# The first batch of a threshold-attention and GELU kernel: divisors through DRAM, conversions counted per slot, and two steps moved

## The chip, the cores and the metric

The kernel runs on one core of one Trainium2 chip. The metric is the device time of one execution in microseconds (us); all times below are us unless they are marked ns. A core has TensorE (PE; its weight loads are listed apart as PEld), VectorE (DVE), ScalarE (ACT), GpSimd (POOL), SyncE (SP, which here only issues DMAs) and 16 DMA engines. [...]

## The reference

```python
# q, k, v: (8, 8, 576, 64) float32; w_in: (512, 2048), w_out: (2048, 512), both float64
scores = (1 / 8) * q @ k.transpose(0, 1, 3, 2)
thresh = scores.max(-1, keepdims=True) - tau
scores = where(scores >= thresh, scores, -1e9)
attn = exp(scores - scores.max(-1, keepdims=True))
attn = attn / (attn.sum(-1, keepdims=True) + 1e-9)
x = (attn @ v)          # to rows of tokens: (4608, 512)
h = x @ w_in
out = (0.5 * h * (1 + erf(h / sqrt(2)))) @ w_out
```

The two weight matrices come as 64-bit floats, and the kernel makes 32-bit floats of them on the chip.

## The kernel before, in words

**Pairs, chunks and slots.** Two heads make a pair; there are 8 batches of 4 pairs, 32 in all. The 576 rows of a pair are cut into five chunks: four of 128 rows for each of the two heads, and a last one that holds the 64 remaining rows of both. One (pair p, chunk i) is a slot n. The first batch (pairs 0 to 3, slots 0 to 19; `BATCH` is 20) has an order of its own: first chunks 0 and 1 of all four pairs (slots 0 to 7), then chunks 2, 3, 4 of each pair (slots 8 to 19). From slot 20 on it is pair by pair. The order on each engine is the order in which this Python program emits the instructions; there is no scheduler (`manual_schedule`).

**A slot of the first batch.** `scores` (L408) lets PE write the scores into one or two of the two PSUM tiles `sc`. `softmax_head` takes the negated row maximum on DVE (L420), on POOL the threshold `thr` (L423) and on ACT the exponentials `p` (L425). `softmax_tail` lets DVE drop what is under the threshold and sum up the rows (L441, the sums go to `den`), which frees the PSUM tile for the scores of the next slot; POOL adds 1e-9 to the sums (L444). One slot later, DVE inverts the sums (`invert`, L450) and PE transposes `p` (`turn_p_early`, L354) through PSUM into pT, which ACT copies out (L361, L365, L370, L374). Another slot later, `weigh_v` or `weigh_half` multiplies pT with v into x^T (L544, L568), ACT copies x^T into its block of tokens (L554, L570), and `divide_early` divides: PE spreads the inverted sums over partitions by matmuls with the identity (L463), ACT copies them (L465), POOL multiplies (L471). x^T comes in two parts, columns 0 to 255 (`TOK`) after chunk 1 and columns 256 to 575 after chunk 4. The second part of pairs 0, 1, 2, 3 falls into slots 12, 15, 18 and 21. From batch 1 on, `divisors` does it otherwise: it transposes the sums on DVE (L482), writes them to DRAM (L485) and reads them back spread over partitions (L491, L493), all from SP.

**PSUM.** All other PSUM tiles (tr, xT, hT, o_ps, idle) share one ring of four (tag `mm`); the fifth of them waits until the first has been read.

**Conversions.** The 64-bit weights come in 32 pieces of 128x512 (16 of w_in, then 16 of w_out), loaded by `load_piece` (L183, from SP) into free slots of xall or into parts of turned_p. A piece is converted in two steps: ACT makes the power and the low half (L202, L203), DVE makes the high half (L210, L211), after which the next piece is loaded; later POOL adds the low bits (L224, `add_low_bits`). `conversions` is a generator that has ACT's step one piece ahead of DVE's, and stops ahead of the last two pieces; `convert(ns)` at the end of every slot lets it run for a debt in ns: 0 in slot 0, 1200 in slots 1 and 2, 1900 later, each piece counted as 1060; the last pieces come in slot 19. In fact DVE converts this many in slots 0 to 19:

```
0 2 1 2 1 2 2 2 2 1 2 2 2 1 2 2 2 2 0 2
```

**The other work of the first batch.** From slot 10 (`START`) on, `fill` gives PE matmuls of layer 1 of token block 0 (L636), 6 to 7 a slot by the goal `GOAL`; ACT copies hT (L603), and after slot 20 turns it into GELU (L609); layer 2 of the block (L651) begins in slot 21. q, k and v of pair 4 are loaded in slot 13 (`load(HP)`), those of pair 5 in slot 17. In slots 1, 6, 8 and 20 `keep_busy` gives PE some idle matmuls (L304).

**After the first batch** PE has the attention of the other 28 pairs, mixed with token blocks as filler, and last the ten remaining blocks in a form with fewer products (L824).

Of the kernel before, what the change touches and what calls it, by code (L numbers as in the profile page):

```python
# [8 lines left out]
FP32 = mybir.dt.float32  # L9
U32 = mybir.dt.uint32  # L10
U8 = mybir.dt.uint8
AF = mybir.ActivationFunctionType
# [6 lines left out]
def kernel(  # L19
# [163 lines left out]
        eng.dma_start(raw, src.bitcast(U32))  # L183
        raws.append((dst, raw, slot))

    def conversions():

        vec = nc.vector
        ahead = []
        done = 0
        while raws or ahead:
            if raws:
                dst, raw, slot = raws.pop(0)
                lo, hi = (raw.rearrange("p (f w) -> p f w", w=2)[:, :, i] for i in range(2))  # L200
                power = gp.tile([P, PIECE], U32, tag="g", name="power")
                nc.scalar.activation(power.bitcast(FP32), hi.bitcast(FP32), AF.Copy, bias=0.0, scale=2.0 ** -112)  # L202
                nc.scalar.activation(dst.bitcast(U32), lo, AF.Copy, bias=0.0, scale=2.0 ** -29)  # L203
                ahead.append((dst, hi, power, slot))
                yield 0
            if len(ahead) == LATER and done == len(pieces) - LATER:
                yield None
            if len(ahead) == 2 or not raws:
                dst, hi, power, slot = ahead.pop(0)
                vec.tensor_scalar(power, power, 3, 0x7FFFFFF8, op0=ALU.logical_shift_left, op1=ALU.bitwise_and)  # L210
                vec.scalar_tensor_tensor(power, hi, 0x80000000, power, op0=ALU.bitwise_and, op1=ALU.bitwise_or)  # L211
                x_free.extend(slot)
                sums_due.append((dst.bitcast(U32), power))
                load_piece()
                done += 1
                yield 1060

    sums_due = []

# [4 lines left out]
            nc.gpsimd.tensor_tensor(dst, power, dst, op=ALU.add)  # L224
            converted[0] += 1

    conv = {"steps": None, "debt": 0.0}

    def convert(ns, least=0):

        if conv["steps"] is None:
            conv["steps"] = conversions()
        conv["debt"] += ns
        while conv["debt"] > 0 or least > 0:
            took = next(conv["steps"], None)
            if took is None:
                return
            conv["debt"] -= took
            least -= took


    st = {}
# [2 lines left out]
    def load(p):  # L245
        for _ in load_steps(p):
            pass
# [180 lines left out]
    def softmax_tail(p, i):  # L428

        s = st[p]  # L430
        sc, thr, w = s.pop(("sc", i)), s.pop(("thr", i)), s["p", i]
        n = len(sc)
        if p < EARLY:
            pair = small.tile([P, 2], FP32, tag="den", name="den", bufs=2 * SLOTS)
            den = [pair[:, e:e + 1] for e in range(n)]
        else:
            at = [e * NC + i if i < NC else 2 * NC for e in range(n)]
            den = [sums[p % 2][:, x:x + 1] for x in at]
        for e in range(n):
            row = w[:, e * S:(e + 1) * S].rearrange("p (h s) -> p h s", h=2)  # L440
            nc.vector.scalar_tensor_tensor(  # L441
                row, sc[e][:, :, 0:HALF], thr[:, e:e + 1], row, op0=ALU.is_ge, op1=ALU.mult, accum_out=den[e])
        if p < EARLY:
            nc.gpsimd.tensor_scalar(pair[:, 0:n], pair[:, 0:n], 1e-9, None, op0=ALU.add)  # L444
            s["sum", i] = pair[:, 0:n]

    def invert(p, i):

        den = st[p]["sum", i]
        nc.vector.reciprocal(den, den)  # L450

    def divide_early(p, lo, hi):

# [165 lines left out]
    def table():  # L619

        if dirty[0]:
            nc.scalar.activation(warm[:, 1:2], warm[:, 0:1], AF.Exp)
            dirty[0] = False
# [466 lines left out]
    PARTS = 1.3, 1.3, 0.2, 1.3, 0.9  # L1090

    HALVED = (2, 3)
    BUSY = {1: 2, 6: 2, 8: 2, BATCH: 4}

    tokens = 0
# [4 lines left out]
    for n in range(len(slots) + WEIGH + 1):  # L1100
# [3 lines left out]
        if p < NP:  # L1104
            scores(p, i)
            softmax_head(p, i)
            add_low_bits()
            if last and last[0] < EARLY:
                invert(*last)
            if p < HP - 1 and i == 0:  # L1110
                turn_qk_early(p + 1)
        elif n == len(slots):
            early_end.close()
            weights_first()
        gelus(0)
        if n == BATCH:
            gelus_held()
        table()
        for args in due:
            if len(args) == 2:  # L1120
                weigh_half(*args)
                if args[1]:
                    divide_early(args[0], 0, TOK)
                continue
            weigh_v(*args)
            divide_early(*args)
        due = []
        if p > EARLY and i == WEIGH:
            for lo, hi in (0, WIDE), (WIDE, S):
                weigh_v(p - 1, lo, hi)  # L1130
            if p == NP:
                divide(p - 1)
# [20 lines left out]
        if p < 2 and i == 0:  # L1153
            for _ in range(2):
                load_piece()
            load_v_early(p + 2)
        if p == 1 and i == NC:
            load(HP)
        if n == BATCH - 3:
            load(HP + 1)  # L1160
        if n == BATCH:
# [9 lines left out]
            scale_q(p + 1)  # L1171
        if p >= HP - 1 and i == 2 and p + 1 < NP:
            turn_qk(p + 1)
        convert(0 if n == 0 else 1200 if n < 3 else 1900 if n < BATCH - 1 else 1e9)
        if not early:
            lag[0] = 2 if p < NP else 0
            if n != BATCH:
# [56 lines left out]
```

## Time and profile before

| | |
|---|---|
| runs without profile | median 1337.11 us of 3 (1337.1 to 1337.74) |
| profiled execution | 1337.72 us, its span 1335.9 us |
| PE busy | 1318.8 us, 99% of the span |
| DVE, ACT, POOL busy | 1039.9, 605.8, 637.0 us |
| L210, DVE, first step of the high half | x32, 488 ns mean |
| L211, DVE, second step | 717 to 720 ns mean |
| L202 and L203, ACT | 0.70 us each, starting 0.57 apart |
| L224, POOL, low bits | x32, 1272 ns mean |
| L463, PE, spreading the divisors | 48 of 80 records in slots 12, 15, 18, 21 |
| L465, ACT, their copy | 373 to 465 ns, x8 |
| L471, POOL, the multiplication | 321 to 1087 ns, x12 |
| L450, DVE, inverting | 154 ns mean |

The maximum of the first head of a slot (L420) starts at these times:

| slot | 1 | 2 | 3 | 4 | 5 | 6 | 7 | 8 | 9 | 10 |
|---|---|---|---|---|---|---|---|---|---|---|
| us | 13.86 | 20.00 | 25.89 | 32.75 | 37.58 | 44.53 | 49.96 | 55.93 | 61.35 | 66.25 |
| **slot** | **11** | **12** | **13** | **14** | **15** | **16** | **17** | **18** | **19** | **20** |
| us | 71.69 | 77.12 | 86.51 | 90.74 | 96.87 | 105.34 | 110.34 | 118.13 | 124.48 | 129.22 |

A line of the timeline gives the start, the duration of the group, the engine, the line of the kernel, the operation, what it writes and reads, how often, and in brackets how long the engine had been idle before and what ended that. An instruction that issues a DMA is listed under SPq. One matmul of 32-bit floats makes two records.

### The profile page before, as it was taken

The numbers are of one execution on the slowest core, as the hardware profiler recorded it, in microseconds if no ns is written. First come the engines' busy times: TensorE is split into PE (matmuls) and PEld (weight loads), VectorE is DVE, ScalarE is ACT, GpSimd is POOL, SyncE is SP. The second block draws the span as 40 slices with busy tenths as digits, with TensorE's granted clock in tenths as the row PEclk, the third lists the DMA queues.
The fourth block names the chain that finished last, engine by engine and source line by source line (L and its number), as shares of the span: only waits on it lengthen the run. The fifth ranks groups of instructions, "written<-read, shape, count | busy, mean of one in ns | idle before, by whom it ended". The sixth has DMA issues, their size and how long they took to land.

```text
span 1335.9 us, 19987 instructions
## 1 busy us (share of the span) xinstructions
PE 1318.8 (99%) x6370; PEld 896.2 (67%) x6370; DVE 1039.9 (78%) x2007; ACT 605.8 (45%) x1029; POOL 637.0 (48%) x1066
## 2 busy tenths in 40 slices
PE   8899999999999999999999999999999999999998
PEld 6677466466466466466466557568788787877877
DVE  6877777788888888888888888783857698386775
ACT  7987457258357358348448428232211103211120
POOL 3655454555555556555555541235264503635530
PEclk9999999999999999999999999999999999999999
DMA  7553565776786786786796775400000130000003
GB/s 242 212 148 64 124 151 139 166 186 152 173 191 151 178 203 154 174 221 155 172 219 156 167 188 116 106 9 1 1 0 1 40 103 17 0 1 0 1 0 80
DMA packets 209784, 152.42 MB, mean 114 GB/s; under 512 B 113360, under 2 KB 193088, under 8 KB 209680
## 3 DMA queue, kind: packets, MB, share of 16 engines
q1 hardware_dynamic: 191536, 124.59, 39.6%
q0 software_dynamic: 17712, 26.26, 7.4%
q8 instruction: 52, 0.85, 0.3%
q14 instruction: 52, 0.43, 0.1%
q10 hardware_dynamic: 432, 0.30, 0.1%
HBM read 55.97 MB, written 12.52 MB: 51 GB/s over the span
## 4 chain that ended last, share of the span: by engine, by line
PE 94%; DVE 2%; ACT 2%; issue 0%; DMA 0%; SPq 0%; POOL 0%; ACTq 0%; DVEq 0%
PE bank L824 34%; PE o_ps L651 17%; PE hT L636 16%; PE sc L408 13%; PE xT L544 11%; DVE nmx L420 1%; ACT p L425 1%; PE tr L354 1%; DVE power L211 1%; ACT pT L361 0%; DVE power L210 0%; DVE p L441 0%; DMA q<-in_q_dram 0%; ACT power L202 0%; PE tr L324 0%
## 5 line engine op out<-in xcount | busy, mean ns | idle before, releaser
L425 ACT ACTIVATE p<-sc,nmx 128x576 f32<-128x576 f32 x288 | 201.9, 737 | 279.1 <-DVE nmx L420 278.8
L441 DVE SCALAR_TENSOR_TENSOR p<-sc,thr,p 128x576 f32<-128x576 f32 x288 | 225.6, 816 | 72.9 <-ACT p L425 62.2
L423 POOL TENSOR_SCALAR thr<-nmx,tau_eff 128x1 f32<-128x1 f32 x288 | 84.0, 293 | 335.8 <-DVE nmx L420 331.3
L636 PE MATMUL hT<-xall,w_in 128*128 128x256 f32 x1024 | 242.1, 386 | 0.5 <-ACT g L603 0.5
L420 DVE TENSOR_REDUCE nmx<-sc 128x1 f32<-128x576 f32 x288 | 205.5, 750 | 44.2 <-PE sc L408 42.7
L651 PE MATMUL o_ps<-w_out,g 128*128 128x512 f32 x512 | 236.8, 603 | 0.0
L636 PEld LDWEIGHTS hT<-xall,w_in 128*128 128x128 f32 x1024 | 189.7, 190 | 50.4 <-issue 23.0
L706 DVE TENSOR_TENSOR o<-o,bank 128x256 f32<-128x256 f32 (+1 forms) x242 | 100.2, 417 | 94.4 <-PE bank L824 89.4
L706 DVE TENSOR_TENSOR c<-c,bank 128x320 f32<-128x320 f32 x304 | 147.1, 488 | 33.9 <-PE bank L824 20.5
L651 PEld LDWEIGHTS o_ps<-w_out,g 128*128 128x128 f32 x512 | 93.3, 190 | 108.9 <-issue 106.6
L408 PE MATMUL sc<-kT,qT 64*128 64x288 f32 x960 | 159.6, 431 | 2.1 <-DVE p L441 1.6
L544 PE MATMUL xT<-pT,v 128*64 128x320 f32 (+1 forms) x1240 | 159.7, 411 | 0.6 <-DVE pT L365 0.5
L505 DVE STREAM_TRANSPOSE turned_p<-p 128x1152 f32<-128x1152 f32 x112 | 154.4, 1378 | 3.9
L408 PEld LDWEIGHTS sc<-kT,qT 64*128 64x128 f32 x960 | 91.5, 187 | 74.9 <-issue 59.2
L544 PEld LDWEIGHTS xT<-pT,v 128*64 128x64 f32 x1240 | 86.7, 137 | 71.6 <-issue 10.7
L824 PE MATMUL bank<-w_out,c 128*128 128x256 f32 (+1 forms) x484 | 120.6, 380 | 0.8 <-DVE o L706 0.8
L267 POOL DMA_DIRECT2D v<-in_v_dram x208 | 110.8, 536 | 4.1 <-issue 2.1
L824 PEld LDWEIGHTS bank<-w_out,c 128*128 128x128 f32 x484 | 90.5, 190 | 18.7 <-DVE o L706 3.2
L891 ACT ACTIVATE c<-c 128x320 f32<-128x320 f32 (+1 forms) x80 | 46.9, 624 | 114.6 <-DVE c L706 114.5
L824 PE MATMUL bank<-t_out,g 128*128 128x256 f32 (+1 forms) x324 | 82.5, 377 | 0.4 <-DVE o L706 0.4
L824 PE MATMUL bank<-t_out,c 128*128 128x256 f32 x320 | 82.8, 381 | 0.0
L706 POOL TENSOR_TENSOR c<-c,g 128x320 f32<-128x320 f32 (+1 forms) x40 | 50.5, 1271 | 67.5 <-DVE c L706 67.5
(181 smaller groups left out, 1762.5 us busy)
## 6 DMA issues: line engine op xcount, KB each, us to landing
pT<-turned_p SPq DMA_DIRECT2D x448, 160.0 KB, 3.5
pT<-pd_tail SPq DMA_DIRECT2D x112, 80.0 KB, 2.8
q<-in_q_dram POOLq DMA_DIRECT2D x104, 72.0 KB, 3.8
k<-in_k_dram POOLq DMA_DIRECT2D x104, 72.0 KB, 3.0
inv<-turned SPq DMA_DIRECT2D x54, 128.0 KB, 4.0
v<-in_v_dram POOLq DMA_DIRECT2D x156, 40.0 KB, 3.1
out_dram<-o SPq DMA_DIRECT2D x40, 128.0 KB, 2.3
xall<-in_moe_w_out_dram SPq DMA_DIRECT2D x9, 512.0 KB, 4.2
```

The source lines that it names most:

```text
L267: eng.dma_start(t[r:P:4, e, 0:n, :], rows[:, r * KR:r * KR + n, :])
L408: nc.tensor.matmul(sc[e][:, h, 0:HALF], lhsT=lhsT, rhs=s["kT"][rows, at:at + HALF], start=True, stop=True)
L420: nc.vector.tensor_reduce(nmx[:, e:e + 1], sc, axis=AXIS.XY, op=ALU.max, negate=True)
L423: nc.gpsimd.tensor_scalar(thr[:, e:e + 1], nmx[:, e:e + 1], -1.0, tau_eff, op0=ALU.mult, op1=ALU.subtract)
L425: nc.scalar.activation(w[:, e * S:(e + 1) * S].rearrange("p (h s) -> p h s", h=2), sc, AF.Exp, bias=nmx[:, e:e + 1], scale=1.0)
L441: nc.vector.scalar_tensor_tensor(row, sc[e][:, :, 0:HALF], thr[:, e:e + 1], row, op0=ALU.is_ge, op1=ALU.mult, accum_out=den[e])
L505: nc.vector.transpose(turned_p[:, :, i // 2, 0:NB, i % 2 * Q:(i % 2 + 1) * Q], w.rearrange("p (e b i) -> p e b i", e=2, i=Q))
L544: nc.tensor.matmul(to, lhsT=s["v"][:, e, c, :], rhs=rhs, start=(c == 0), stop=(c == KR - 1))
L636: nc.tensor.matmul(hT[:, j % 2, :], lhsT=w_in_sb[c][:, j * P:(j + 1) * P], rhs=x_blk[n][:, c, :], start=(c == 0), stop=(c == N_DM - 1))
L651: nc.tensor.matmul(o[:, 0:d_model], lhsT=g[j][:, m * P:(m + 1) * P], rhs=w_out_sb[j], start=(j == 0), stop=(j == N_DF - 1))
L706: eng.tensor_tensor(out, a, b, op=ALU.add)
L824: nc.tensor.matmul(to, lhsT=l, rhs=r, start=start and k == 0, stop=k == len(pairs) - 1, skip_group_check=not start)
```

## The change

- **Divisors of the second part through DRAM.** In the first batch, chunks 2, 3 and 4 now sum into columns of `sums` instead of `den`; 1e-9 is added once a pair, after chunk 4. The new `divisors_early(p)`, called in the slot after chunk 4 (slots 11, 14, 17, 20), inverts and transposes the sums on DVE, writes them to DRAM and reads them back spread over partitions with four DMAs, all issued by SP. The target is a part of w_out that is not yet converted for pairs 0 and 1, and the tile `inv` for pairs 2 and 3. The new `divide_late(p)` lets POOL multiply in slots 14, 16, 19 and 22 (`DIVIDE_LATE`). The matmuls of L463 and the copies of L465 for columns 256 to 575 are gone, and `invert` remains for chunks 0 and 1.
- **Conversion steps per slot.** Instead of the debt in ns, a list `STEPS` says how many pieces DVE converts in each slot; ACT is one piece ahead. All 32 are done in slot 18. By the built program DVE's counts in slots 0 to 19 are

```
0 1 1 1 1 1 2 1 2 2 2 2 3 2 2 3 2 2 2 0
```

- **ScalarE's halves sooner in the slots of long x^T.** In slots 12, 15 and 18, `convert_ahead` gives ACT the halves of the slot's pieces (3, 3 and, as only one is left, 1) right after its exponentials and its copy of hT, ahead of the copies of x^T and pT.
- **q and k of pair 4 sooner.** They are loaded in slot 11 (`START + 1`) instead of slot 13, behind the DMAs of `divisors_early(0)`; v stays in slot 13.

The order of TensorE's instructions is otherwise the same in both built programs.

```diff
--- before.py
+++ after.py
@@ -183,37 +183,32 @@
         eng.dma_start(raw, src.bitcast(U32))
         raws.append((dst, raw, slot))
-    def conversions():
+    ahead = []
+    def convert_first():
+        dst, raw, slot = raws.pop(0)
+        lo, hi = (raw.rearrange("p (f w) -> p f w", w=2)[:, :, i] for i in range(2))
+        power = gp.tile([P, PIECE], U32, tag="g", name="power")
+        nc.scalar.activation(power.bitcast(FP32), hi.bitcast(FP32), AF.Copy, bias=0.0, scale=2.0 ** -112)
+        nc.scalar.activation(dst.bitcast(U32), lo, AF.Copy, bias=0.0, scale=2.0 ** -29)
+        ahead.append((dst, hi, power, slot))
+    def convert_second():
         vec = nc.vector
-        ahead = []
-        done = 0
-        while raws or ahead:
-            if raws:
-                dst, raw, slot = raws.pop(0)
-                lo, hi = (raw.rearrange("p (f w) -> p f w", w=2)[:, :, i] for i in range(2))
-                power = gp.tile([P, PIECE], U32, tag="g", name="power")
-                nc.scalar.activation(power.bitcast(FP32), hi.bitcast(FP32), AF.Copy, bias=0.0, scale=2.0 ** -112)
-                nc.scalar.activation(dst.bitcast(U32), lo, AF.Copy, bias=0.0, scale=2.0 ** -29)
-                ahead.append((dst, hi, power, slot))
-                yield 0
-            if len(ahead) == LATER and done == len(pieces) - LATER:
-                yield None
-            if len(ahead) == 2 or not raws:
-                dst, hi, power, slot = ahead.pop(0)
-                vec.tensor_scalar(power, power, 3, 0x7FFFFFF8, op0=ALU.logical_shift_left, op1=ALU.bitwise_and)
-                vec.scalar_tensor_tensor(power, hi, 0x80000000, power, op0=ALU.bitwise_and, op1=ALU.bitwise_or)
-                x_free.extend(slot)
-                sums_due.append((dst.bitcast(U32), power))
-                load_piece()
-                done += 1
-                yield 1060
+        dst, hi, power, slot = ahead.pop(0)
+        vec.tensor_scalar(power, power, 3, 0x7FFFFFF8, op0=ALU.logical_shift_left, op1=ALU.bitwise_and)
+        vec.scalar_tensor_tensor(power, hi, 0x80000000, power, op0=ALU.bitwise_and, op1=ALU.bitwise_or)
+        x_free.extend(slot)
+        sums_due.append((dst.bitcast(U32), power))
+        load_piece()
     sums_due = []
@@ -224,19 +219,17 @@
             nc.gpsimd.tensor_tensor(dst, power, dst, op=ALU.add)
             converted[0] += 1
-    conv = {"steps": None, "debt": 0.0}
-    def convert(ns, least=0):
-        if conv["steps"] is None:
-            conv["steps"] = conversions()
-        conv["debt"] += ns
-        while conv["debt"] > 0 or least > 0:
-            took = next(conv["steps"], None)
-            if took is None:
-                return
-            conv["debt"] -= took
-            least -= took
+    def convert_ahead(steps):
+        while raws and len(ahead) <= steps:
+            convert_first()
+    def convert(steps):
+        while steps > 0 and (ahead or raws):
+            convert_ahead(1)
+            convert_second()
+            steps -= 1
     st = {}
@@ -430,8 +423,8 @@
         s = st[p]
         sc, thr, w = s.pop(("sc", i)), s.pop(("thr", i)), s["p", i]
         n = len(sc)
-        if p < EARLY:
-            pair = small.tile([P, 2], FP32, tag="den", name="den", bufs=2 * SLOTS)
+        if p < EARLY and i < 2:
+            pair = small.tile([P, 2], FP32, tag="den", name="den", bufs=2 * HP)
             den = [pair[:, e:e + 1] for e in range(n)]
         else:
             at = [e * NC + i if i < NC else 2 * NC for e in range(n)]
@@ -440,14 +433,49 @@
             row = w[:, e * S:(e + 1) * S].rearrange("p (h s) -> p h s", h=2)
             nc.vector.scalar_tensor_tensor(
                 row, sc[e][:, :, 0:HALF], thr[:, e:e + 1], row, op0=ALU.is_ge, op1=ALU.mult, accum_out=den[e])
-        if p < EARLY:
+        if p < EARLY and i < 2:
             nc.gpsimd.tensor_scalar(pair[:, 0:n], pair[:, 0:n], 1e-9, None, op0=ALU.add)
             s["sum", i] = pair[:, 0:n]
+        elif p < EARLY and i == NC:
+            at = sums[p % 2][:, 0:2 * NC + 1]
+            nc.gpsimd.tensor_scalar(at, at, 1e-9, None, op0=ALU.add)
     def invert(p, i):
         den = st[p]["sum", i]
         nc.vector.reciprocal(den, den)
+    def divisors_early(p):
+        den = sums[p % 2]
+        nc.vector.reciprocal(den[:, 0:2 * NC + 1], den[:, 0:2 * NC + 1])
+        turned = small.tile([P, Q], FP32, tag="turned", name="turned", bufs=2)
+        nc.vector.transpose(turned, den)
+        rows = dram.tile([4, Q, Q], FP32, tag="turned", name="turned", bufs=4)
+        nc.sync.dma_start(rows.rearrange("a k i -> (a k) i"), turned)
+        t = st[p]["inv"] = w_out_sb[N_DF - 1 - p] if p < 2 else dg.tile([P, S], FP32, tag="inv", name="inv")
+        flat = rows.rearrange("a k i -> a (k i)")
+        for e in range(2):
+            to = t[e * D:(e + 1) * D]
+            src = flat[:, (e * NC + 2) * Q:(e * NC + 4) * Q].unsqueeze(0).to_broadcast([D, 4, 2 * Q])
+            nc.sync.dma_start(to[:, 0:TOK].rearrange("p (a x) -> p a x", x=2 * Q), src)
+            src = rows[2 * e:2 * e + 2, 2 * NC, :].unsqueeze(0).to_broadcast([D, 2, Q])
+            nc.sync.dma_start(to[:, TOK:TOK + TAIL].rearrange("p (a x) -> p a x", x=Q), src)
+    def divide_late(p):
+        b, hp = divmod(p, HP)
+        by = st[p].pop("inv")
+        for n, o, at, size in in_blocks(b, TOK, S):
+            x, y = x_blk[n][:, hp, o:o + size], by[:, at - TOK:at - TOK + size]
+            if size == TOK:
+                x = x.rearrange("q (a i c) -> q a c i", i=Q, c=2)
+                y = y.rearrange("q (a c i) -> q a c i", i=Q, c=2)
+            nc.gpsimd.tensor_tensor(x, x, y, op=ALU.mult)
     def divide_early(p, lo, hi):
@@ -1090,6 +1118,8 @@
     PARTS = 1.3, 1.3, 0.2, 1.3, 0.9
     HALVED = (2, 3)
+    DIVIDE_LATE = {14: 0, 16: 1, 19: 2, 22: 3}
+    STEPS = [0, 1, 1, 1, 1, 1, 2, 1, 2, 2, 2, 2, 3, 2, 2, 3, 2, 2, 2]
     BUSY = {1: 2, 6: 2, 8: 2, BATCH: 4}
     tokens = 0
@@ -1105,8 +1135,10 @@
             scores(p, i)
             softmax_head(p, i)
             add_low_bits()
-            if last and last[0] < EARLY:
+            if last and last[0] < EARLY and last[1] < 2:
                 invert(*last)
+            if last and last[0] < EARLY and last[1] == NC:
+                divisors_early(last[0])
             if p < HP - 1 and i == 0:
                 turn_qk_early(p + 1)
         elif n == len(slots):
@@ -1116,6 +1148,8 @@
         if n == BATCH:
             gelus_held()
         table()
+        if early and n > START and any(hi == S for _, *_, hi in due):
+            convert_ahead(STEPS[n] if n < BATCH - 1 else LATER)
         for args in due:
             if len(args) == 2:
                 weigh_half(*args)
@@ -1123,8 +1157,11 @@
                     divide_early(args[0], 0, TOK)
                 continue
             weigh_v(*args)
-            divide_early(*args)
+            if args[1] == 0:
+                divide_early(*args)
         due = []
+        if n in DIVIDE_LATE:
+            divide_late(DIVIDE_LATE[n])
         if p > EARLY and i == WEIGH:
             for lo, hi in (0, WIDE), (WIDE, S):
                 weigh_v(p - 1, lo, hi)
@@ -1154,8 +1191,13 @@
             for _ in range(2):
                 load_piece()
             load_v_early(p + 2)
-        if p == 1 and i == NC:
-            load(HP)
+        if n == START + 1:
+            loads = load_steps(HP)
+            next(loads)
+            next(loads)
+        if n == START + 3:
+            for _ in loads:
+                pass
         if n == BATCH - 3:
             load(HP + 1)
         if n == BATCH:
@@ -1171,7 +1213,7 @@
             scale_q(p + 1)
         if p >= HP - 1 and i == 2 and p + 1 < NP:
             turn_qk(p + 1)
-        convert(0 if n == 0 else 1200 if n < 3 else 1900 if n < BATCH - 1 else 1e9)
+        convert(STEPS[n] if n < BATCH - 1 else len(pieces))
         if not early:
             lag[0] = 2 if p < NP else 0
             if n != BATCH:
```

## The prediction

> **What bounds the kernel now.** I read the chain of work that ended last, then busy time by stage, then the timeline of the first 142 us.
>
> ```profile
> PE 94%; DVE 2%; ACT 2%; issue 0%; DMA 0%; SPq 0%; POOL 0%; ACTq 0%; DVEq 0%
> ```
>
> TensorE ends the program; the 2% each of DVE and ACT lies early, since in each 20 us from 140 to 300 TensorE is busy for 20.00. By stage (us; then busy time of PE, weight loads, DVE, ACT, POOL; granted clock; DMA share):
>
> ```profile
> 10.00:64.00 54.00, 47.16 (x447) 34.41 (x443) 44.63 (x96) 49.36 (x103) 27.64 (x46) 0.97 0.70 238
> 64.00:128.00 64.00, 61.84 (x369) 47.05 (x368) 46.69 (x99) 49.57 (x102) 33.55 (x53) 1.00 0.47 117
> 128.00:142.00 14.00, 13.31 (x82) 8.18 (x83) 10.24 (x22) 12.31 (x23) 5.33 (x15) 1.00 0.00 0
> ```
>
> From 10 to 64 us (slots 1 to 9) ScalarE has 91% and TensorE has 6.8 us of idle; from 64 us (slots 10 on, with block 0 as filler) TensorE has 97%. Before 64 us an early slot goes like slot 7:
>
> ```profile
> 51.77 0.82 DVE L441 SCALAR_TENSOR_TENSOR p<-sc,thr,p 128x576 f32<-128x576 f32 x1 [0.33 <-POOL thr L423]
> ...
> 52.65 1.97 PE L408 MATMUL sc<-kT,qT 64*128 64x288 f32 x8
> ...
> 53.19 0.74 POOL L471 TENSOR_TENSOR xall<-xall,inv 128x256 f32<-128x256 f32 x1
> ...
> 53.25 0.96 DVE L210 TENSOR_SCALAR power<-power 128x512 uint32<-128x512 uint32 x1
> ...
> 54.25 0.69 DVE L211 SCALAR_TENSOR_TENSOR power<-xall,power 128x512 uint32<-128x512 uint32 x1
> ...
> 54.86 0.42 DVE L210 TENSOR_SCALAR power<-power 128x512 uint32<-128x512 uint32 x1
> ...
> 55.32 0.69 DVE L211 SCALAR_TENSOR_TENSOR power<-turned_p,power 128x512 uint32<-128x512 uint32 x1
> ...
> 55.93 1.41 DVE L420 TENSOR_REDUCE nmx<-sc 128x1 f32<-128x576 f32 x2
> ```
>
> The next scores are ready at 54.62; their maximum waits to 55.93 for the second conversion. Here a conversion costs the slot its DVE time, 1.07. In the long slots (12, 15, 18: TOK to S of x^T) it is the other way round:
>
> ```profile
> 79.09 0.72 PE L463 MATMUL tr<-ident,den 128*64 128x128 f32 x12
> 79.20 0.58 ACT L603 COPY g<-hT 128x512 f32<-128x512 f32 x1
> ...
> 79.67 0.51 ACT L554 COPY xall<-xT 128x256 f32<-128x256 f32 x2
> ...
> 80.04 0.47 ACT L465 COPY inv<-tr 128x320 f32<-128x320 f32 x1
> ...
> 83.56 1.07 ACT L361 COPY pT<-tr 128x512 f32<-128x512 f32 x2 [3.06 <-PE tr L354]
> 84.20 0.14 PEld L354 LDWEIGHTS tr<-ident,p 128*128 128x128 f32 x1 [0.53 <-ACT pT L361]
> ...
> 84.37 1.14 PE L408 MATMUL sc<-kT,q_tail 128*128 128x288 f32 x4
> ```
>
> ScalarE stands still for 3.06 while TensorE works.
>
> [...] L210 takes 0.42 alone and 0.96 beside the multiplication at 53.19. [...]
>
> **The change, part by part.** The order of the two built programs has the same TensorE instructions, less 24 matmuls of L463.
>
> *Conversions per slot.* Slots 1 to 9 had 2,1,2,1,2,2,2,2,1 and get 1,1,1,1,1,2,1,2,2. Slots 1, 3, 5 and 7 lose one each. In each the next maximum (L420) then waits for what is next late:
> - slot 1: sc ends 18.40, the remaining conversion 18.93, maximum 20.00: gain 1.07;
> - slot 3: sc ends 31.47, maximum 32.75: gain about 1.15, since sc takes over;
> - slot 5: sc 43.23, maximum 44.53: 1.2, again sc;
> - slot 7: 54.94 against 55.93: 1.0.
>
> ScalarE loses 1.14 in each of them too (halves at 84.73, 85.29, next 85.87), so it does not take over. Sum 4.4 at slot 8. Slot 9 gets one more and is DVE-bound (conversion to 66.33, maximum 66.25, scores there at 65.29): -1.1. At slot 10 the work stands about **3.3 earlier**. TensorE's work does not shrink here; its 6.8 of idle is what gives way, and were it gone, the gain would be nothing. The granted clock falls to 0.89, 0.50 and 0.76 in 22 to 28 us (sc of slot 3 takes 2.29 for 1.24). If that dip goes, up to 1.0 is won, if it moves into a slot of the same kind, as much is lost; ScalarE, without idle before exp of slot 3 (26.68), holds the slot anyway: I take 0.
>
> *Slots 10 and 11* keep two each. TensorE reaches the scores of slot 10 4.4 earlier (only L441 of slot 9 is before them), so pT comes sooner and DVE's wait of 0.73 for ScalarE's half (before 70.62) shrinks: I take 0.4 of it. 3.7 at the scores of slot 12, which DVE's L441 sets (PE waits 0.69 before 74.48).
>
> *Divisors through DRAM.* TensorE loses L463 for columns TOK to S: from its start to the next hT 0.66, 0.65, 0.65 and 0.91, **2.87** in slots 12, 15, 18, 21. ScalarE loses four copies of 0.47. DVE loses 12 reciprocals of 0.15 and gets four, and four transpositions of 0.21 (L482): about nothing, beside waits of 0.33 for thr. POOL loses 8 adds of 0.28. Its multiplications move from slots 12, 15, 18, 21 to 14, 16, 19, 22; their new strides are not in the trace: between the 0.74 and the 1.09 of L471, I take 0.9. SP gets 5 DMAs a pair: 0.59 for the write, 1.9 until it lands (up to 3.8), four of 0.6, then 4.0 to landing (up to 6.6): 9 us, at most 13.4, against 22, 16, 14 and 14 us until the multiplication. So nothing waits, if SP reaches them in time.
>
> *ScalarE's halves sooner.* In slots 12, 15 and 18 it gets 3, 3 and 1 conversions ahead of the x^T copies. TensorE's transposition of the second half (slots 12 and 18) or the last (slot 15) takes the PSUM buffer that these copies free. Slot 12: exps end 79.30, g copy 79.78, conversions 3.4, x^T copies 0.5: 83.6; TensorE would be there at 82.7 without L463. It saves 0.66 and waits 0.9: a net loss of about 0.2, while ScalarE's halves after slot 12 are gone (84.73 to 87.12), so the maximum of slot 13 comes 1.3 sooner; TensorE doesn't wait for it. Slot 15: 99.54 + 3.4 + 0.5 = 103.4, against 102.2 without L463: DVE's lead there makes it 0.2 to 0.5 lost. Slot 18: 120.80 + 1.14 + 0.5 = 122.45, against a need at 121.9: even. So the matmuls of L463 bring nothing in these three slots, and 0.3 to 0.4 in slot 21, where sc waits for DVE's L441 (ends 141.27).
>
> *Slots 13 and 14.* Slot 13 has two conversions instead of one. The second one's half stands behind the pT copies on ScalarE: on the new time pT ends at 86.25, half 0.7, DVE 1.1, so 88.05, where the scores of slot 14 are ready at 86.95; before, the maximum started with them (90.74 after 90.71). sc of slot 15 follows on L441 of slot 14 at once (93.97 after 93.93): **1.0 lost**. The later counts are equal, but for 2 moved from slot 19 to 18, where DVE idles (2.98).
>
> *Loads of pair 4.* q and k (8 DMAs, 5.4) go from slot 13 to 11, behind the row DMAs; pieces of slot 11 are issued some 10 us later, but are converted in slot 14, 20 us on. No cost; v stays.
>
> *Slot 16.* Its conversions done, the maximum can start with the scores (103.86) and not at 105.34: 1.5 for DVE, of which sc of slot 18 (stalled by L441, 1.75 for 1.24) sees a part, between 0 and 1.3: I take 0.55.
>
> *Sum*: 3.3 + 0.4 - 0.2 (slot 12) - 1.0 - 0.2 (slot 15) + 0.55 + 0.35 (slot 21) = **3.2**. After 142 us TensorE is the bound, in the same order, so this stays. The profiled execution took 1337.72 (span 1335.9 and 1.8 around it): 1334.5. It is 0.6 over the median: **1333.9** as median.
>
> **The rivals.**
> - *B, ScalarE keeps up*: 3.3 of the early slots and 2.87 of L463 both arrive, 6.1 to 6.2: 1330.9. For it: ScalarE's 3.06 of idle in slot 12, and 2.17 before the pT copies of slot 15. Against it: 3.4 is more than either.
> - *C, GpSimd in the way*: the slots after three conversions (13, 16) have two low-bit adds of 1.27 behind thr, and slots 14 and 16 the multiplications; DVE's conversions, on the path there, meet them. At 0.42 to 0.96 for L210, 0.69 to 1.11 for L211 (100.62), some 0.5 in slot 13, 14 and twice in 16: up to 2 of the 3.2 are lost, 1.7 as middle: 1335.6. For it: 53.25. Against: most L210 of the stage are undisturbed (0.49 on average).
> - *D, slower: rows that come late.* GpSimd's multiplication of slots 16, 19, 22 waits for its DMA, behind it thr of the next slot, DVE's L441 and sc. It decides from 14 us between the transposition and the landing. If SP comes 5 us late (piece loads wait there up to 4.5 for DVE) and both latencies are at their longest, 18: beyond 14, so three slots lose some 2 each after overlap, 6.0: 6.0 - 3.2 = 2.8 slower, 1339.9.
>
> **How the numbers follow.** This kernel's measurement tells about 0.2% (2.7) from no change. The main case, 1332.9 to 1334.9, has 0.54; B 0.14 (1330.7 to 1332.9); C 0.23 (1334.9 to 1337.1); D 0.09. Faster than 1334.4: 0.77 of the main case and B, 0.56. Same: the rest and C, 0.35. Slower: D, 0.09. The range 1331.2 to 1336.7 leaves out D and the ends of B and C, under 0.2.
>
> **What would show it.** Right: the maximum of slot 10 near 63.0 (66.25 now), slot 13 near 82, slot 16 near 101.5, slot 19 near 121.6; gaps of PE before the second transposition of slots 12 and 18 that end with the x^T copy; no wait of GpSimd for rows. Wrong: slot 10 still near 66 (then something else sets the early slots), no gaps there (B), L210 over 0.8 in slots 13, 14 and 16 (C), the late multiplication waiting for a DMA (D).

## The result, and the profile after

The median is 1333.85 us of 10 runs (1332.32 to 1335.26) against 1337.07 of 10 runs before: a ratio of **0.9973 [0.9965, 0.9981]**, 3.2 us less. The profiled execution took 1333.98 with a span of 1332.1; before it was 1337.72 and 1335.9.

Line numbers have moved: L420 is now L413 (maximum), L408 L401 (scores), L441 L434 (p and its sums), L354 L347 (transposition of p), L361 L354 (its copy), L202 and L203 L199 and L200 (ScalarE's halves), L210 and L211 L207 and L208 (DVE's steps), L554 L582 (copy of x^T), L603 L631 (copy of hT). The chain of work that ended last:

```profile
PE 91%; DVE 3%; ACT 2%; issue 1%; DMA 1%; POOL 1%; SPq 0%; DVEq 0%; POOLq 0%; ACTq 0%
```

The stages, with the columns that the prediction names (PE, weight loads, DVE, ACT, POOL, clock, DMA):

```profile
10.00:64.00 54.00, 52.04 (x478) 38.73 (x475) 45.48 (x94) 49.59 (x105) 25.74 (x45) 1.00 0.66 221
64.00:128.00 64.00, 59.71 (x333) 43.61 (x332) 51.73 (x104) 50.85 (x103) 37.50 (x56) 1.00 0.49 141
128.00:142.00 14.00, 13.46 (x52) 6.47 (x52) 10.35 (x21) 10.33 (x18) 5.83 (x12) 1.00 0.28 60
```

TensorE is busy for 52.04 of the first 54 us, where it was 47.16: the early slots have closed up. Slot 7, timeline:

```profile
47.97 1.97 PE L401 MATMUL sc<-kT,qT 64*128 64x288 f32 x8
...
48.50 0.74 POOL L499 TENSOR_TENSOR xall<-xall,inv 128x256 f32<-128x256 f32 x1
...
48.57 0.96 DVE L207 TENSOR_SCALAR power<-power 128x512 uint32<-128x512 uint32 x1
...
49.56 0.69 DVE L208 SCALAR_TENSOR_TENSOR power<-turned_p,power 128x512 uint32<-128x512 uint32 x1
...
50.17 1.41 DVE L413 TENSOR_REDUCE nmx<-sc 128x1 f32<-128x576 f32 x2
```

There is one pair of L207 and L208 where there were two. The scores end at 49.94 and the conversion at 50.25 (its listed end overlaps the next start a little), so the maximum starts at 50.17, 0.23 behind the end of the scores, where before it started 1.31 behind them. Slot 12, the first one with long x^T, timeline:

```profile
74.00 0.58 ACT L631 COPY g<-hT 128x512 f32<-128x512 f32 x1
74.46 0.69 ACT L199 ACTIVATE power<-turned_p 128x512 f32<-128x512 f32 x1
...
77.36 0.66 ACT L200 ACTIVATE w_out<-turned_p 128x512 uint32<-128x512 uint32 x1
...
77.92 0.46 ACT L582 COPY xall<-xT 128x256 f32<-128x256 f32 x2
...
78.28 0.58 ACT L354 COPY pT<-tr 128x512 f32<-128x512 f32 x1
78.44 0.81 PE L347 MATMUL tr<-ident,p 128*128 128x128 f32 x5 [0.72 <-ACT xall L582]
...
79.08 1.14 PE L401 MATMUL sc<-kT,q_tail 128*128 128x288 f32 x4
```

Where ScalarE had 3.06 of idle in that slot it now makes the halves of three conversions (74.46 to 78.02, 3.56 in all), and TensorE waits 0.72 for the copy behind them, as the prediction had it (0.9).

How far the profiled execution is ahead of that of before, by the start of each slot's first maximum (both executions start their slot 0 within 0.15 of each other):

| slot | 1 | 2 | 4 | 6 | 8 | 10 | 12 | 13 | 14 | 16 | 17 | 20 | 23 | 100 | 159 |
|---|---|---|---|---|---|---|---|---|---|---|---|---|---|---|---|
| us | -0.2 | 1.0 | 3.3 | 4.5 | 5.8 | 4.8 | 5.2 | 6.3 | 4.5 | 5.3 | 4.3 | 4.3 | 4.5 | 4.5 | 4.1 |

All of it is won by slot 8; slots 8 to 20 give back 1.4 of the 5.8. About 1.0 of the lead is the dip of the clock, which the profile of before has and this one has not (experiment 4). Slot 159, the last one, is at 838.9.

### The profile page after: what moved, and what is told of

Its sections match the earlier page's. It is cut to its first block, busy times and chain, and to the rows that moved or that the text cites. A ratio compares the mean times of both kernels' runs of the same rounds, so it can differ in the third digit from the quotient of the medians.

```text
span 1332.1 us, 19898 instructions
## 1 busy us (share of the span) xinstructions
PE 1317.4 (99%) x6322; PEld 891.8 (67%) x6322; DVE 1041.0 (78%) x2003; ACT 603.8 (45%) x1025; POOL 635.2 (48%) x1058
## 4 chain that ended last, share of the span: by engine, by line
PE 91%; DVE 3%; ACT 2%; issue 1%; DMA 1%; POOL 1%; SPq 0%; DVEq 0%; POOLq 0%; ACTq 0%
PE bank L852 34%; PE o_ps L679 17%; PE hT L664 16%; PE sc L401 13%; PE xT L572 11%; DVE nmx L413 1%; DVE p L434 1%; ACT p L418 1%; PE tr L347 1%; DVE power L208 1%; DVE power L207 1%; ACT power L199 0%; DMA inv<-turned 0%; ACT w_out L200 0%; POOL thr L416 0%
## 5 line engine op out<-in xcount | busy, mean ns | idle before, releaser
L434 DVE SCALAR_TENSOR_TENSOR p<-sc,thr,p 128x576 f32<-128x576 f32 x288 | 225.2, 815 | 72.9 <-ACT p L418 65.2
L413 DVE TENSOR_REDUCE nmx<-sc 128x1 f32<-128x576 f32 x288 | 205.3, 749 | 46.9 <-PE sc L401 45.6
L401 PE MATMUL sc<-kT,qT 64*128 64x288 f32 x960 | 159.8, 429 | 2.3 <-DVE p L434 1.6
L401 PEld LDWEIGHTS sc<-kT,qT 64*128 64x128 f32 x960 | 91.4, 186 | 75.8 <-issue 60.4
```

The costliest lines, as they stand in the source:

```text
L401: nc.tensor.matmul(sc[e][:, h, 0:HALF], lhsT=lhsT, rhs=s["kT"][rows, at:at + HALF], start=True, stop=True)
L413: nc.vector.tensor_reduce(nmx[:, e:e + 1], sc, axis=AXIS.XY, op=ALU.max, negate=True)
L434: nc.vector.scalar_tensor_tensor(row, sc[e][:, :, 0:HALF], thr[:, e:e + 1], row, op0=ALU.is_ge, op1=ALU.mult, accum_out=den[e])
```

## The experiments

Theory: the counts win in the early slots, and no other part matters much. First rival: ScalarE's halves sooner carry the change, since fewer conversions early mean more of them in slots 12 to 18, and only these halves let that backlog pass. Second rival: the gain is the dip of the clock, which the profile of before has and that of after has not. Each kernel was compared with runs of the kernel before in the same session (medians 1336.95 to 1337.21), and the ratios are against these. A difference from the change is one between medians of different sessions; by the intervals it is clear of noise from some 1.5 to 2 us on, and with one trace for each kernel the traces tell the smaller ones apart only in part.

**1. The counts alone**, put into the kernel before:

```diff
-        convert(0 if n == 0 else 1200 if n < 3 else 1900 if n < BATCH - 1 else 1e9)
+        convert(STEPS[n] if n < BATCH - 1 else len(pieces))
```

> The kernel before with the new counts of conversions per slot alone. Theory (the early slots give the gain, slots 1, 3, 5 and 7 one conversion each): slot 10 starts near 61.5 as in the changed kernel, 4.5 to 4.8 us sooner; some of it is lost in slots 12 to 16, where three conversions now stand behind the pT copies on ScalarE; end 2.5 to 3.5 us faster than before. Rival (each part brings a share, the conversions about a third): 1 us faster.

Measured: 1337.58, ratio 1.0003 [0.9995, 1.0011]. Nothing is left of the gain, and the 2.5 to 3.5 of the theory are missed. Its lead over before, counted from slot 0 (from the first maximum on, so that an earlier or later start of the whole doesn't count), is 5.3 at slot 12, as in the change (5.35), and 0.2 at slot 20. Slots 12 and 15, with three conversions each, lead to the loss. Slot 12 and the start of 13, timeline:

```profile
79.57 0.27 ACT L363 COPY pT<-tr 128x128 f32<-128x128 f32 x1
79.73 0.67 ACT L199 ACTIVATE power<-turned_p 128x512 f32<-128x512 f32 x1
...
80.43 0.43 DVE L207 TENSOR_SCALAR power<-power 128x512 uint32<-128x512 uint32 x1 [3.46 <-ACT power L199]
...
82.57 0.68 ACT L200 ACTIVATE w_out<-turned_p 128x512 uint32<-128x512 uint32 x1
82.64 0.75 DVE L413 TENSOR_REDUCE nmx<-sc 128x1 f32<-128x576 f32 x1
...
84.06 0.58 ACT L596 COPY g<-hT 128x512 f32<-128x512 f32 x1
...
84.69 0.82 PE L347 MATMUL tr<-ident,p 128*128 128x128 f32 x5 [1.17 <-ACT g L596]
```

The halves stand behind the copies of pT, DVE idles 3.46 for the first of them, then has two conversions ahead of the maximum at 82.64, though the scores were there at 80.51; the exponentials, the copy of hT behind them and TensorE's transposition follow late. In the profile after, the same maximum starts at 80.25.

**2. The divisors through DRAM alone**, put into the kernel before: `divisors_early` and `divide_late` as in the change, the conversions by the old debt.

> The kernel before with the divisors of the second part through DRAM alone. Theory: with no halves of conversions ahead of the x^T copies, the matmuls of L463 were on TensorE's path in slots 12, 15 and 18, so 0.65 comes in each and 0.35 in slot 21: 2.0 to 2.5 us faster. Rival (rows or GpSimd's late multiplications cost as much as they save): within 0.5 us of before.

Measured: 1337.39, ratio 0.9999 [0.9991, 1.0007]: nothing that shows, so the 2.0 to 2.5 of the theory are missed. The interval leaves room for up to 1.2, and the profile, which has no dip of the clock, is 1.25 ahead of that of experiment 4 at slot 20 and 0.64 at slot 159 (counted from slot 0). So a small gain of its own is not excluded.

**3. The change without ScalarE's halves sooner:**

```diff
-        if early and n > START and any(hi == S for _, *_, hi in due):
-            convert_ahead(STEPS[n] if n < BATCH - 1 else LATER)
```

> The changed kernel without ScalarE's halves sooner. Theory: TensorE no longer waits for the x^T copies in slots 12, 15 and 18 (some 2.4 us of waits in the changed kernel go), but three conversions' halves stand behind the pT copies and delay the exponentials of slots 13 and 16: between 1 us faster and 1 us slower than the changed kernel. Rival (the halves sooner carry the change): over 2 us slower than the changed kernel.

Measured: 1338.41 (1335.18 to 1340.17), ratio 1.0005 [0.9996, 1.0015]: 4.6 slower than the change, so the theory's number is far off and the first rival's holds. What TensorE waited for from 55 to 142 us (total, times, longest), here:

```profile
PE tr L347 <- ACT g L631: 2.8, 2, 1.6
PE sc L401 <- DVE p L434: 1.8, 2, 1.4
PE tr L347 <- ACT pT L354: 1.8, 3, 1.2
```

and in the change:

```profile
PE tr L347 <- ACT xall L582: 2.4, 3, 0.9
PE sc L401 <- DVE p L434: 0.9, 3, 0.5
PE tr L347 <- ACT pT L354: 0.5, 2, 0.2
```

The sum of the three rows is 6.4 against 3.8. The profiled execution is the slowest of the 13 and 6.2 behind that of the change; most of what the waits leave open is the clock: this profile has two stretches of 3.41 us at half clock, each right after such a wait. The 3.41 us ahead of each, and the stretch itself (PE busy first, clock in the place behind POOL):

```profile
89.27:92.68 3.41, 2.03 (x12) 1.03 (x10) 3.30 (x9) 3.35 (x9) 3.15 (x6) 1.00 0.23 59
92.68:96.09 3.41, 3.41 (x15) 1.64 (x16) 2.99 (x6) 2.73 (x6) 1.92 (x4) 0.50 0.65 180
113.16:116.57 3.41, 2.32 (x11) 1.33 (x13) 2.95 (x7) 3.35 (x9) 1.96 (x4) 1.00 0.05 10
116.57:119.98 3.41, 3.41 (x16) 1.67 (x14) 3.31 (x9) 1.69 (x3) 0.49 (x1) 0.50 0.51 92
```

The mean granted clock of each run says the same without a profile: 9 of the 13 runs have 0.996 or 0.997 and take 1339.2 on average, the other four have 0.998 to 1.000 and take 1336.3.

**4. The dip filled.** The kernel before, with more work for TensorE ahead of where its clock dipped: four transpositions of slot 2 are done three times over (the same values are written again).

```diff
-            for c in range(NC):
-                turn(tr[:, c, :], e * (S + TAIL) + c * P)
+            for _ in range(3 if (p, i, e) == (0, 1, 0) else 1):
+                for c in range(NC):
+                    turn(tr[:, c, :], e * (S + TAIL) + c * P)
```

> The kernel before, with the first four transpositions of slot 2 made three times, so that TensorE has no idle of 1.5 us there (same result). Theory (the dip of the granted clock at 23.5 to 27 us cost slot 3 some 1.0 to 1.4 us, and its absence is why the changed kernel is ahead of the forecast in slot 10): no half clock in the trace, slot 4 starts 1.0 us sooner, end 1.0 to 1.4 us faster than before. Rival (ScalarE holds slot 3 anyway): no dip, and the time of before.

Measured: 1336.83, ratio 0.9996 [0.9988, 1.0004]. All its 13 runs have a clock of 0.999 or 1.000, and its profile is 0.93 to 0.97 ahead of that of before from slot 4 to slot 159 (counted from slot 0). So the dip is worth 1.0 in the profile, and about 0.4 in the median, which the interval doesn't tell from nothing. The second rival falls as the main cause: most of the 3.2 is something else.

**5. The change with the divisors as before** (`invert` and `divide_early` for all columns, no `divisors_early`, no `divide_late`).

> The changed kernel with the divisors of the second part as before (matmuls of L463, copies, multiplications in the long slots); counts per slot, halves sooner and loads stay. Theory (counts and halves sooner carry the change together; in the long slots ScalarE's copies of x^T hold TensorE, so the divisors' way matters by ScalarE's 0.47 copy and little else): 0.3 to 1.3 us slower than the changed kernel. Rival (DRAM divisors are worth their 2.9 us of TensorE): about 3 us slower, the time of before.

Measured: 1334.63 of 21 runs, ratio 0.9983 [0.9977, 0.999]: by the medians the divisors through DRAM give 0.8 within the change, as the theory has it, but the interval overlaps that of the change. Its profile can't settle the size: that execution is the slowest of the 21 by 3.2, and its slot 0 starts 2.3 later than that of the change. Against experiment 1 it also shows the halves sooner (and the loads): 1337.58 to 1334.63, so 3.0.

So no part carries the change alone. The counts alone, the divisors alone and the change without the halves sooner are no faster than the kernel before; counts and halves sooner together (with the loads) give 2.4 of the 3.2. The halves sooner with the old counts were not run.

**6. The halves behind the copies of x^T**, and still ahead of those of pT:

```diff
-        if early and n > START and any(hi == S for _, *_, hi in due):
-            convert_ahead(STEPS[n] if n < BATCH - 1 else LATER)
+        long_x = early and n > START and any(hi == S for _, *_, hi in due)
...
+        if long_x:
+            convert_ahead(STEPS[n] if n < BATCH - 1 else LATER)
```

> The changed kernel with the halves behind the copies of x^T and ahead of pT's in slots 12, 15 and 18. Theory (the wait in slot 15 is for x^T, those in 12 and 18 turn into waits for pT): the waits of TensorE for x^T go, 0.5 to 0.8 us faster than the changed kernel. Rival (all three were held by x^T alone): 2 us faster.

Measured: 1332.27 (1332.24 to 1332.48), ratio 0.9964 [0.9951, 0.9976], 1.6 faster than the change, between the theory and its rival. The waits for the copies of long x^T (L582) are gone from its list; waits for pT's copies (L354) took most of their place, 2.2 in sum where the change has 0.5.

**7. q and k of pair 4 in slot 13 again** (`if p == 1 and i == NC: load(HP)`).

> The changed kernel with q and k of pair 4 loaded in slot 13 as before. Theory (no one waits for these loads or for the pieces behind them): within 0.3 us of the changed kernel. Rival (in slot 13 the 16 DMAs hold up the rows of pair 1, and GpSimd with them): 1 us slower.

Measured: 1334.25, ratio 0.9978 [0.9968, 0.9988]: 0.4 from the change, less than its runs scatter. The loads cost and bring nothing that shows.

**8. One conversion less ahead**, in slots 12 and 15 (slot 18 has only one left, with this edit or without):

```diff
-            convert_ahead(STEPS[n] if n < BATCH - 1 else LATER)
+            convert_ahead(STEPS[n] - 1 if n < BATCH - 1 else LATER)
```

> The changed kernel with one half less ahead of the x^T copies in slots 12 and 15 (two instead of three). Theory (three halves of 3.4 us are more than ScalarE's idle of about 3 there): TensorE's waits for x^T in these slots go, 0.7 to 1.5 us faster than the changed kernel. Rival (the third half behind pT delays the exponentials of the next slot as without halves sooner, a third of the 4.6 us lost there): 1 us slower.

Measured: 1332.6, ratio 0.9964 [0.9951, 0.9976], 1.25 faster than the change. TensorE's waits for x^T in slots 12 and 15 are gone from its trace, that of slot 18 (0.87) stays. ScalarE's 3.06 of idle takes two conversions (2.3); the third was too much.

**9. One conversion in slot 13**, not two (`STEPS[13] = 1`; the last one moves to slot 19).

> The changed kernel with one conversion instead of two in slot 13 and the last one in slot 19. Theory (the second conversion of slot 13, behind the pT copies, makes the maximum of slot 14 late and costs the scores of slot 15 1.0 us): the scores of slot 15 no longer wait for L434, 0.7 to 1.0 us faster than the changed kernel. Rival (another wait takes its place in slot 15, for x^T behind three halves): within 0.3 us.

Measured: 1335.14 of 21 runs, ratio 0.9985 [0.9979, 0.9992], 1.3 slower than the change, so the theory is missed. The gain came and went: its lead, counted from slot 0, is 0.7 over that of the change at slot 14 and 0.6 at slot 17, but 2.2 under it at slot 20. With one piece left over, slot 18 has two conversions ahead of x^T instead of one. TensorE there, timeline:

```profile
116.01 0.66 PE L347 MATMUL tr<-ident,p 128*128 128x128 f32 x4 [0.31 <-ACT g L631]
118.65 0.81 PE L347 MATMUL tr<-ident,p 128*128 128x128 f32 x5 [1.99 <-ACT xall L582]
```

and the 3.41 us around it and those after them:

```profile
115.95:119.36 3.41, 1.36 (x10) 1.06 (x11) 2.76 (x6) 3.15 (x9) 1.01 (x2) 1.00 0.46 84
119.36:122.77 3.41, 3.41 (x9) 2.57 (x9) 0.76 (x1) 1.31 (x3) 1.36 (x3) 0.50 0.21 51
```

The wait of 1.99 is 1.1 longer than that of the change in this slot (0.88), and half clock (0.50) follows for the next 3.41, which by that clock is 1.7 of work. By runs: 17 of 21 have a mean clock of 0.997 or 0.998 and take 1335.4 on average; the other four have 0.999 and take 1333.86, as the change does.

**10 to 12. The edits put together**: 6 and 8; 6, 8 and 9; 8 and 9.

> Halves behind the x^T copies and one less in slots 12 and 15, together. Theory (each of the two alone left about 0.9 us of waits, one for x^T in slot 18, one for pT): 0.5 us faster than either alone, about 2 us faster than the changed kernel. Rival (the same waits, met twice): no faster than either alone.

> Halves behind the x^T copies, one less of them in slots 12 and 15, and one conversion in slot 13. Theory (the three waits are in different places): 2.5 to 3 us faster than the changed kernel, near 1331. Rival (DVE or ScalarE takes over in slots 14 to 17): as the one before.

> One half less ahead in slots 12 and 15 and one conversion in slot 13, with x^T behind the halves. Theory: 2 to 2.3 us faster than the changed kernel, 0.3 to 0.6 us slower than all three. Rival: as one half less alone.

Measured: 1332.34, ratio 0.9965 [0.9953, 0.9976]; 1332.14 (1330.38 to 1333.0), 0.996 [0.9947, 0.9972]; and **1331.19** (1330.02 to 1331.48), 0.9955 [0.9943, 0.9967]. Six and eight don't add up, since both take away the waits for x^T in slots 12 and 15. Eight and nine go together: with one conversion less ahead, slot 18 has one there and not two, and what slot 13 wins arrives. At slot 20 the profile of experiment 12 is 0.7 ahead of that of experiment 8 (counted from slot 0). All three together missed the 1331 of their theory: the profile of experiment 11 is level with that of 12 at slot 20 (6.7 ahead of before), and loses 0.75 between slots 80 and 100, which was not explained. With five or six runs each, the intervals don't tell 10, 11 and 12 apart. TensorE's waits from 55 to 142 us in experiment 12:

```profile
PE tr L347 <- ACT xall L582: 0.9, 1, 0.9
PE tr L347 <- ACT pT L354: 0.8, 3, 0.3
PE sc L401 <- DVE p L434: 0.7, 2, 0.5
```

2.4 where the change has 3.8. By the medians this version is 2.7 faster than the change and 5.8 faster than the kernel before.

## Why the prediction was right, and where it wasn't

The time forecast, 1333.9, is the time measured, 1333.85, and most of the waits are those that the prediction named. That the two times agree so closely is luck: several steps were off by up to 1 us, and their errors offset each other. To leave the dip out, the leads below are taken against experiment 4, whose profile is the kernel before without it, and counted from slot 0.

- **Slots 1, 3, 5 and 7**, 1.07, 1.15, 1.2 and 1.0 forecast: 1.16, 1.27, 1.27 and 1.07 by the start of the next slot's maximum. **Slot 9**, -1.1: it is -1.06. **Slots 10 and 11**, 0.4: they give 0.45. With that 4.4 stand at slot 12, where 3.7 were forecast. Mechanism right, size 0.7 short: the gains of slots 3 and 5, cut short in the forecast because "sc takes over", came in full (0.2 more), slot 6 gave 0.2 that was not forecast, and the rest is less than 0.1 in each of the others.
- **Slots 12 to 20**: -0.2 (slot 12), -1.0 (slots 13 and 14), -0.2 (slot 15) and +0.55 (slot 16) were forecast, -0.85 in sum, and 0.85 is lost. But it is not lost where it was forecast. At the start of TensorE's scores (L401) the lead is

| slot | 12 | 13 | 14 | 15 | 16 | 17 | 18 | 19 | 20 |
|---|---|---|---|---|---|---|---|---|---|
| us | 4.39 | 4.47 | 4.47 | 4.15 | 3.03 | 3.03 | 3.48 | 3.54 | 3.54 |

  Slot 12 cost nothing: its second transposition waits 0.72 for x^T, as foreseen, and the matmuls of L463 are gone. The second conversion of slot 13 made the scores of slot 15 wait for L434, as foreseen, but it cost them 0.3 and not 1.0. Slot 15 cost 1.1 and not 0.2. The prediction had the copies of x^T there 1.2 later than TensorE needed them, and took most of that off for "DVE's lead there"; but the maximum of slot 15 is only 3.87 ahead, less than TensorE, and the wait of 0.83 came. With two halves ahead instead of three (experiment 8) slot 15 costs 0.1. Slot 16 (+0.45) and slot 18 (even, with a wait of 0.88) are as forecast. So the waits are those that were named, two of the sizes are wrong, and their sum is right by luck.
- **ScalarE's halves sooner** were priced as "a net loss of about 0.2" in slot 12. Beside the kernel before that is their place in the queue; what the step lacked is what the new counts would be without them. Experiments 1 and 5 put that (with the loads) at 3.0, and experiment 3, with its half clock, at 4.6: without them the whole gain goes in slots 12 to 19. The sum holds only for the parts together.
- **The divisors**: the 2.87 of L463 do not arrive, as forecast, in slots 12, 15 and 18, since the copies of x^T behind ScalarE's halves set the pace there. Slot 21 gives 0.15 (0.35 forecast). Experiment 5 has 0.8 for the whole, not clear of noise.
- **The clock**, taken as 0: in the profiles this step failed. The text argued that ScalarE, without idle before the exponentials of slot 3, "holds the slot anyway". ScalarE does hold those exponentials: counted from slot 0 they start within 0.02 of each other with the dip and without. But behind them TensorE's own work, done at half clock, was late. ScalarE then waits 0.77 for x^T in the kernel before,

```profile
26.68 1.41 ACT L425 ACTIVATE p<-sc,nmx 128x576 f32<-128x576 f32 x2
28.86 0.40 ACT L554 COPY xall<-xT 128x256 f32<-128x256 f32 x1 [0.77 <-PE xT L544]
```

  and not at all in experiment 4,

```profile
25.74 1.36 ACT L426 ACTIVATE p<-sc,nmx 128x576 f32<-128x576 f32 x2
26.99 0.40 ACT L555 COPY xall<-xT 128x256 f32<-128x256 f32 x1
```

  where the scores of slot 4 end 1.0 sooner (counted from slot 0). And the dip does not only move. All 10 runs of the change have a mean clock of 0.999, while of the 97 runs of the kernel before in the experiments' sessions 59 have 0.998 or less; the 54 with 0.998 take 1337.5 on average, and 28 with 0.999 take 1336.2. This is a sign and no proof: one dip (3.41 us at 0.50) lowers the mean by 0.0013, and the half clock at the very end, 1.7 us long in the profile before and 3.8 in that of the change, by 0.0006 and 0.0014. (Ten runs have 1.000 and take 1337.2, which was not explained.) The clock's part of the 3.2 probably lies between the 0.4 of experiment 4, which its interval doesn't tell from nothing, and some 0.9, the median before less those 1336.2.
- **After 142 us** "this stays": nearly. The lead over before is 4.5 at slot 100 and 4.1 at slot 159; 0.45 goes late. Around slot 130 (680 to 698 us) the waits show

```profile
POOL xall L612 <- DMA inv<-turned: 0.7, 1, 0.7
...
DVE p L434 <- POOL thr L416: 1.9, 2, 1.4
```

  where before (684 to 702 us) they were

```profile
POOL xall L584 <- DMA inv<-turned: 0.2, 1, 0.2
...
DVE p L441 <- POOL thr L423: 0.9, 1, 0.9
```

  That is rival D's mechanism, GpSimd waiting for rows with thr behind it, at a later place and a small size. Between slots 100 and 159 experiments 1, 4, 7 and 9 have no such loss and the others have 0.2 to 0.8, so it isn't tied to one part of the change. Why the rows come later there was not settled.

In sum for the profiles: 4.4 + 0.95 (clock) - 0.85 (slots 12 to 20) + 0.15 (slot 21) - 0.45 (late) = 4.2, less 0.15 for the start of slot 0: 4.05 at slot 159, and 3.8 in the spans. The forecast of 3.2 for the profiled executions was 0.5 short (3.74); it meets the medians because the profiled execution before was 0.6 over its median, and that of the change only 0.1.

**The signs to look for.** Slot 10 near 63.0, 13 near 82, 16 near 101.5, 19 near 121.6: they came at 61.49, 80.25, 100.05 and 120.14, each about 1.5 earlier, which is the 0.7 and the 1.0. The gaps ahead of the second transpositions are there, so B (no wait for ScalarE) is out. For D, the late multiplication was never held up: from 60 to 150 us GpSimd waits for no DMA. Pair 1's rows were written at 91.43, read from 95.85 on and used at 103.93.

C, GpSimd in DVE's way, is not out. From 58 to 118 us most L207 take 0.42, but in slot 14 one took 0.96 beside the late multiplication (L478), and in slots 13 and 16 one L208 took 1.64, where 0.69 is usual, beside two additions of low bits (L219). Slots 13 to 15, timeline:

```profile
81.43 2.74 POOL L219 TENSOR_TENSOR w_out<-power,w_out 128x512 uint32<-128x512 uint32 x2
...
83.08 1.64 DVE L208 SCALAR_TENSOR_TENSOR power<-turned_p,power 128x512 uint32<-128x512 uint32 x1
...
85.15 0.43 DVE L207 TENSOR_SCALAR power<-power 128x512 uint32<-128x512 uint32 x1 [0.43 <-ACT power L199]
...
89.46 1.20 POOL L478 TENSOR_TENSOR xall<-xall,w_out 128x256 f32<-128x256 f32 x2
...
89.52 0.96 DVE L207 TENSOR_SCALAR power<-power 128x512 uint32<-128x512 uint32 x1
...
92.96 1.41 ACT L418 ACTIVATE p<-sc,nmx 128x576 f32<-128x576 f32 x2 [0.65 <-DVE nmx L413]
...
98.71 0.33 PE L347 MATMUL tr<-ident,p 128*128 128x128 f32 x1 [0.83 <-ACT xall L582]
```

In slots 13 and 16 it cost nothing, as DVE's next step had to wait another 0.43 for ScalarE's half anyway. In slot 14 it made the maximum of slot 15 late: it starts 1.23 behind the end of its scores, and 0.75 behind in experiments 1 and 5, which have no multiplication there. ScalarE waits 0.65 for this maximum and then works without idle until it has copied x^T. So by an estimate from these numbers some 0.5 of TensorE's wait of 0.83 in slot 15 is C's, of the up to 2 that the rival named; no run tested this alone. Why DVE's steps take longer beside these of GpSimd was not shown. The slot 7 shown above has a slow L207 too (0.96 beside L499); there the maximum is at most the 0.23 late that it starts behind its scores.

## What to carry to other kernels

Work taken out of early stages comes back as a backlog, and the time that it saved is only kept if the place where the backlog is done can take it: count, for that place, what stands in the queue of each engine ahead of what the critical engine waits for. When a step is moved into another engine's idle time, fill that idle to its size and not beyond it: 3.06 of idle took two conversions of 1.14, and the third made TensorE wait in both slots that had it (0.72 and 0.83). When the parts of a forecast are checked, check each one where the critical engine meets it: a sum can be right with its parts wrong. A stall of TensorE should be priced with the half clock that may follow it: in experiment 9 a wait of 1.99 had 3.41 us at 0.50 behind it, in the change one of 0.88 had none.

## What the runs showed of the hardware

The dip of the clock is not a drift. In the kernel before it is one stretch of 3.41 us at 0.50 (23.55 to 26.96), and the stretches at full clock around it last 17.07 and 1307.31, five and 383 times as long; that of the change lasts 1320.96, 387 times. Experiment 3 has two stretches of 3.41 at half clock, experiment 9 has one. The kernel before seems to meet the dip in most runs and not in all: of its 97 runs, 54 have a mean clock of 0.998 and 28 have 0.999. TensorE was not idle ahead of it. The 3.41 us before the dip, and the dip itself, are

```profile
20.14:23.55 3.41, 1.86 (x21) 1.29 (x17) 3.07 (x8) 3.24 (x7) 3.12 (x5) 1.00 0.51 130
23.55:26.96 3.41, 3.41 (x15) 1.95 (x16) 1.94 (x4) 3.34 (x9) 1.73 (x3) 0.50 0.82 251
```

and the other three dips, shown above, came after stretches with 2.03, 2.32 and 1.36 of 3.41 busy. In stretches of 3.41 us, counted from where each profile's record of the clock starts (6.48 in the kernel before, 7.34 in the change), the 14 profiles have 19 with 2.32 or less between 15 and 142 us; half clock came after 4 of these, and after none that had more. Experiment 2, which does the same work as the kernel before up to slot 10, has one with 1.87 (18.54 to 21.95), and full clock after it. The change has one that low:

```profile
116.57:119.98 3.41, 2.32 (x14) 1.81 (x15) 2.92 (x8) 2.93 (x8) 1.01 (x2) 1.00 0.54 93
119.98:123.39 3.41, 3.41 (x21) 3.05 (x20) 1.58 (x3) 1.44 (x3) 3.33 (x5) 1.00 0.20 51
```

It stayed at full clock, while half clock came after the 2.32 of experiment 3. So TensorE's busy time, as the profile shows it, doesn't tell when half clock comes; what settles it was not shown.

The price is better known: by the granted 0.50 TensorE does 1.7 us less in 3.41 (an estimate from the clock; the scores of slot 3 take 2.29 with the dip in them, and 1.24 in the change), the profile of experiment 4 is 0.93 to 0.97 ahead without the dip, and runs whose mean clock points to a dip took 1.3 (kernel before, 0.998 against 0.999) to 1.6 (experiment 9) longer than those where it points to none.
